# A fixed order on every engine, and local-branch work cut into steps with set lags, in an attention kernel for training

## The chip, the cores and the metric

The kernel runs on one core of a Trainium2 chip. The metric is device time of one execution in microseconds (us). Before the change the median of three runs was 1798.34 us (1797.06 to 1816.73).

Engines in the text: PE multiplies matrices, PEld loads its weights, DVE and ACT do elementwise work, POOL does elementwise work too (adding 128x432 numbers took it 1102 ns, and DVE 603 ns, in the kernel before), and SP issues DMA transfers. PSUM is the memory into which PE writes; the attention phase uses eight of its banks.

## The reference

One encoder block with an attention branch and a local branch (a gated depthwise convolution), forward, and then the gradients of the input and of all seven weights. B = 2, T = 4000, D = 144, five taps, all bf16.

```python
def _fwd_reference(x, w_qkv, w_att_out, w_mlp_in, dw_csgu, w_mlp_out, dw_merge, w_merge):
    xa = _layernorm(x, axis=-1)
    q, k, v = split(xa @ w_qkv)                       # shortened
    p = _softmax(q @ k^T * D ** (-0.5))               # shortened
    glob = (p @ v) @ w_att_out                        # shortened
    h = _gelu(xa @ w_mlp_in)                          # shortened
    u, g = (h[..., :D].copy(), h[..., D:].copy())
    g = _layernorm(g, axis=-1)
    gc = depthwise_conv(g, dw_csgu)                   # 5 taps along T; shortened
    loc = (u * gc) @ w_mlp_out                        # shortened
    ...                                               # merge convolution, projection, residual
# reference(): jax.vjp of this with grad_out; returns the output and eight gradients
```

## The kernel before

Each of the two batches goes through four phases: a head, attention, merge and output, and the gradient of x. One last phase finishes the weight gradients. The change touches the attention phase alone. It goes through 32 rows of 128 tokens, with four *units* per row. A unit makes scores for 1000 columns: eight matmuls into two banks `pS` and two banks `pD`, two exponentials on ACT (`Pm`), two products on DVE (`Sm`). The probabilities and products of older rows are transposed by DMA and multiplied into `y`, and the gradient for the columns is summed through `X` ("fills", two banks, emptied by ACT and POOL or by DVE).

Between these units the kernel runs the local branch, one chain for every pair of rows: `pr`, `ph` (twice), a gelu and norm chain that gives `gn_t`, transposes of it (`pm`, put into `gnC`), a convolution `pc`, transposes of its gradient (`dgC`), the convolution back (`pc` again, read by ACT as `dgf`), and for every two pairs a weight gradient `pw` (twice). **All of these PE steps, and `pj`, which prepares the attention's operands, use the one PSUM bank `ps_f`.** Each must therefore wait until ACT or DVE has emptied the bank of the step before.

```python
def pD(p):                                   # convolution back
    ...
    pc = dgC.conv(p, True)
    for q in range(2):
        nc.scalar.activation(dg[:, q, :], pc[:, q, :], ACT.Copy, scale=rs[:, q:q + 1], accum_out=s12[:, 0, q:q + 1])
    ...
# the local branch is a list of events with times in units; R7 = 7 units per pair
for p in range(NBK // 2):
    t = R7 * p
    ev += [(t, pR, (p,)), (t + 1, pH, (p, 0)), (t + 2, pH, (p, 1)), (t + 2.5, pG, (p,)),
           (t + 9, lambda p: gnC.put(p, gn_t[p]), (p,)), (t + 14, ld_dug, (p,)), (t + 18, pC, (p,)),
           (t + 21, lambda p: dgC.put(p, dgc_t[p]), (p,)), (t + 31, pD, (p,))]
for q in range(NGR):
    ev += [(2 * R7 * q + 24, ld_tap, (q,)), (2 * R7 * q + 31.4, pW, (q, 0)), (2 * R7 * q + 32.4, pW, (q, 1))]
...
# in phase_attn
fills = {(0, 0): 0, (0, 1): 1, (1, 0): 2, (2, 0): 3, (2, 1): 4, (3, 0): 5, (4, 0): 6, (4, 1): 7, (5, 0): 8, (6, 0): 9, (6, 1): 10}
with tc.manual_schedule(engines={mybir.EngineType.PE}):      # PE alone in program order
    for i in range(NBK + 2):
        pr, half = i // 2 - 1, i % 2
        for c2 in range(4):
            if i < NBK:
                unit(i, c2)                  # scores; exponentials and Sm at high priority
            if i < NBK and c2 >= 2:
                flip(i, c2 - 2)              # DMA transposes of P and of Sm
            for place in range(2):
                ...                          # a fill, and at place 0 yz(i - 2, c2)
            if c2 == 3 and i < NBK:
                row_end(i)                   # 1/sum, Qs, br, and Bt
            ...                              # pj at units of its own
            while ev and ev[0][0] < 4 * i + c2 + 1:
                _, fn, a = ev.pop(0)         # all events that are due, one after another
                fn(*a)
```

Only PE follows the program's order here. The order on ACT, DVE, POOL and SP is chosen by a scheduler when the kernel is built.

Of the kernel before, what the change touches and what calls it, by code (L numbers as in the profile page):

```python
# [7 lines left out]
BF = mybir.dt.bfloat16  # L8
# [6 lines left out]
D = 144  # L15
# [1521 lines left out]
def local_steps(k, W, b, S, es, ps):  # L1537
# [9 lines left out]
    R, hs, sq, h_t, gn_t, gp_t, rstd, dug, dgc_t, dh_t, gtap = {}, {}, {}, {}, {}, {}, {}, {}, {}, {}, {}  # L1547
    id_ = W.ident

    def pR(p):  # L1550
        R[p] = wk.tile([128, 256], BF, tag="R", name="R")
        pr = ps.tile([128, 2, 128], BF, tag="f", name="pr")
        for j in range(2):
            nc.tensor.transpose(pr[:, j, :], S.xaa[:, 2 * p + j, 16:D], id_[:])
        nc.scalar.copy(R[p][:], pr[:].rearrange("p a b -> p (a b)"))
        hs[p] = wk.tile([128, 2, 2 * D], BF, tag="hs", bufs=1, name="hs")
        sq[p] = wk.tile([128, 2, 2 * D], BF, tag="sq", bufs=1, name="sq")

    def pH(p, j):
        i = 2 * p + j  # L1560
        ph = ps.tile([128, 2 * D], F32, tag="f", name="ph")
        nc.tensor.matmul(ph[:], S.xaT[:, i * 128:(i + 1) * 128], W.Wi2[:, 0, :], start=True, stop=False)
        nc.tensor.matmul(ph[:], R[p][:, j * 128:(j + 1) * 128], W.Wi2[:, 1, :], start=False, stop=True)
        nc.scalar.copy(hs[p][:, j, :], ph[:])
        nc.scalar.activation(sq[p][:, j, :], ph[:], ACT.Square)
        if j == 1:
            R.pop(p)

    def pG(p):

        h_ = h_t[p] = wk.tile([128, 2, 2 * D], BF, tag="h_t", bufs=4, name="h_t")
        gn_t[p] = wk.tile([128, 2, D], BF, tag="gn_t", bufs=6, name="gn_t")
        gp_t[p] = wk.tile([128, 2, 2 * D], BF, tag="gp_t", bufs=6, name="gp_t")
        rstd[p] = sm.tile([128, 2], F32, tag="rstd", bufs=6, name="rstd")
        x_, s_ = hs.pop(p), sq.pop(p)
        a_ = wk.tile([128, 2, 2 * D], BF, tag="a_", bufs=1, name="a_")
        nc.gpsimd.tensor_scalar(a_[:], s_[:], K0 * K1, K0, op0=ALU.mult, op1=ALU.add)
        nc.vector.tensor_tensor(a_[:], a_[:], x_[:], op=ALU.mult)
        nc.scalar.activation(a_[:], a_[:], ACT.Tanh)
        nc.vector.tensor_scalar(a_[:], a_[:], 0.5, 0.5, op0=ALU.mult, op1=ALU.add)  # L1580
        nc.vector.tensor_tensor(h_[:], a_[:], x_[:], op=ALU.mult)
        norm_rows(k, W, sm, gn_t[p], h_[:, :, D:2 * D], rstd[p], 2, "g")
        t3 = wk.tile([128, 2, 2 * D], BF, tag="t3", bufs=1, name="t3")
        nc.gpsimd.tensor_scalar(t3[:], s_[:], 6 * K0 * K1, 2 * K0, op0=ALU.mult, op1=ALU.add)
        oq = wk.tile([128, 2, 2 * D], BF, tag="oq", bufs=1, name="oq")
        nc.gpsimd.tensor_scalar(oq[:], a_[:], -1.0, 1.0, op0=ALU.mult, op1=ALU.add)
        nc.gpsimd.tensor_tensor(oq[:], oq[:], h_[:], op=ALU.mult)
        nc.vector.tensor_tensor(oq[:], oq[:], t3[:], op=ALU.mult)
        nc.vector.tensor_tensor(gp_t[p][:], oq[:], a_[:], op=ALU.add)
        nc.sync.dma_start(S.gn_d[2 + p * 256:2 + (p + 1) * 256, :].rearrange("(j p) c -> p j c", p=128), gn_t[p][:])  # L1590

    def ld_dug(p):
        dug[p] = wk.tile([128, 2, D], BF, tag="dug", name="dug")
        nc.sync.dma_start(dug[p][:], S.dug_d[:, 2 * p:2 * p + 2, :])

    def ld_tap(q):
        gtap[q] = on.tile([128, 4, 5, D], BF, tag="gtap", name="gtap")
        gn_taps(k, gtap[q], S.gn_d, q, nc.sync)

    def pC(p):  # L1600
        pc = gnC.conv(p, False)
        gc = wk.tile([128, 2, D], BF, tag="gc", bufs=1, name="gc")
        nc.scalar.copy(gc[:], pc[:])
        u_, d_ = h_t.pop(p)[:, :, 0:D], dug.pop(p)
        dgc = dgc_t[p] = wk.tile([128, 2, D], BF, tag="dgc", bufs=4, name="dgc")
        dh_t[p] = wk.tile([128, 2, 2 * D], BF, tag="dh", bufs=3, name="dh")
        ug = wk.tile([128, 2, D], BF, tag="ug", name="ug")
        du = wk.tile([128, 2, D], BF, tag="du", bufs=1, name="du")
        nc.vector.tensor_tensor(dgc[:], d_[:], u_, op=ALU.mult)
        nc.vector.tensor_tensor(du[:], d_[:], gc[:], op=ALU.mult)  # L1610
        nc.vector.tensor_tensor(ug[:], u_, gc[:], op=ALU.mult)
        nc.vector.tensor_tensor(dh_t[p][:, :, 0:D], du[:], gp_t[p][:, :, 0:D], op=ALU.mult)
        nc.sync.dma_start(S.ug_d[:, 2 * p:2 * p + 2, :], ug[:])

    def pW(q, half):

        pw = ps.tile([128, 384], F32, tag="f", name="pw")
        for j in range(4):
            d_ = dgc_t[2 * q + j // 2]
            fl = dict(stop=(j == 3), skip_group_check=True)  # L1620
            if half == 0:
                nc.tensor.matmul(pw[:], d_[:, j % 2, 0:128], gtap[q][:, j, 0:3, 0:128], start=(j == 0), **fl)
            else:
                nc.tensor.matmul(pw[:, 0:256], d_[:, j % 2, 0:128], gtap[q][:, j, 3:5, 0:128], start=(j == 0), **fl)
                nc.tensor.matmul(pw[:, 256:336], d_[:, j % 2, 16:D], gtap[q][:, j, :, 128:D], start=False, **fl)
        w = 384 if half == 0 else 336
        ds = dWs[:, half * 384:half * 384 + w]
        nc.vector.tensor_tensor(ds, pw[:, 0:w], ds, op=ALU.add)
        if half == 1:
            for t in (2 * q, 2 * q + 1):  # L1630
                dgc_t.pop(t)

    def pD(p):
        dh, gn, rs = dh_t.pop(p), gn_t.pop(p), rstd.pop(p)
        s12 = sm.tile([128, 2, 2], F32, tag="s12", name="s12")
        dg = wk.tile([128, 2, D], BF, tag="dgf", name="dgf")
        cc = wk.tile([128, 2, D], BF, tag="cc", bufs=1, name="cc")
        jk = on.tile([128, D], BF, tag="jk", name="jk")
        pc = dgC.conv(p, True)
        for q in range(2):  # L1640
            nc.scalar.activation(dg[:, q, :], pc[:, q, :], ACT.Copy, scale=rs[:, q:q + 1], accum_out=s12[:, 0, q:q + 1])
        for q in range(2):
            nc.vector.scalar_tensor_tensor(jk[:], dg[:, q, :], 1.0, gn[:, q, :], op0=ALU.mult, op1=ALU.mult, accum_out=s12[:, 1, q:q + 1])
        n12 = sm.tile([128, 2, 2], F32, tag="n12", name="n12")
        nc.vector.tensor_scalar(n12[:], s12[:], -1.0 / D, None, op0=ALU.mult)
        for q in range(2):
            nc.gpsimd.tensor_scalar(cc[:, q, :], gn[:, q, :], n12[:, 1, q:q + 1], n12[:, 0, q:q + 1], op0=ALU.mult, op1=ALU.add)
        nc.vector.tensor_tensor(dg[:], dg[:], cc[:], op=ALU.add)
        nc.vector.tensor_tensor(dh[:, :, D:2 * D], dg[:], gp_t.pop(p)[:, :, D:2 * D], op=ALU.mult)
        nc.sync.dma_start(S.dh_d[:, 2 * p:2 * p + 2, :], dh[:])  # L1650

    def taps():
        dc = sm.tile([128, 2, 5], F32, tag="dc", name="dc")
# [6 lines left out]
    ev = []  # L1660
    R7 = 7
    for p in range(NBK // 2):
        t = R7 * p
        ev += [(t, pR, (p,)), (t + 1, pH, (p, 0)), (t + 2, pH, (p, 1)), (t + 2.5, pG, (p,)),
               (t + 9, lambda p: gnC.put(p, gn_t[p]), (p,)), (t + 14, ld_dug, (p,)), (t + 18, pC, (p,)),
               (t + 21, lambda p: dgC.put(p, dgc_t[p]), (p,)), (t + 31, pD, (p,))]
    for q in range(NGR):
        ev += [(2 * R7 * q + 24, ld_tap, (q,)), (2 * R7 * q + 31.4, pW, (q, 0)), (2 * R7 * q + 32.4, pW, (q, 1))]
    ev.append((1e9, taps, ()))
    ev.sort(key=lambda e: e[0])  # L1670
    return ev


def phase_attn(k, W, b, S):
# [3 lines left out]
    with ExitStack() as es:  # L1678
# [20 lines left out]
        def jit(g, step):  # L1699
            r = slice(g * 4, g * 4 + 4)  # L1700
            if step == 0:
                jt[g] = [xp.tile([128, 4, 128], BF, tag=t_, name=t_) for t_ in ("QTm", "BTm", "QBr")]
                for off, src in ((0, S.Q_t), (32, S.B_t), (64, S.Q_t), (96, S.B_t)):
                    nc.gpsimd.tensor_scalar(QB[:, :, off:off + DR], src[:, r, 128:D], 1.0, 0.0, op0=ALU.mult, op1=ALU.add)
            src = (S.Q_t[:, r, 0:128], S.B_t[:, r, 0:128], QB[:])[step]
            pj = ps_f.tile([128, 4, 128], BF, tag="f", name="pj")
            for j in range(4):
                nc.tensor.transpose(pj[:, j, :], src[:, j, :], id_[:])
            nc.scalar.copy(jt[g][step][:], pj[:])
# [25 lines left out]
        def flip(i, h):  # L1735

            pb = i % NP
            for key, src in (("PT", P), ("ST", Sm)):
                t = st[key, i, h] = ab.tile([128, 16, 128], BF, tag=key, bufs=3, name=key)
# [451 lines left out]
```

## Time and profile before

| | before |
|---|---|
| time, median | 1798.34 us |
| attention stage (first exponential to last `X` matmul), first and second batch | 649, 651 us |
| everything else (from the trace's span) | 512 us |
| PE gaps in a stage | 109, 106 us |
| of these ahead of local steps | 91, 89 us |

A gap is the time from the latest end of any matmul or weight load on PE to the next start. I worked the gaps out from the trace's records.

First, five lines of the page of the kernel before. The second is each engine's busy time; the next three are the span in 40 slices with busy shares in tenths, where PEclk is the granted clock in tenths.

```profile
span 1811.2 us, 41290 instructions
...
PE 1401.6 (77%) x15366; PEld 1046.6 (58%) x15366; DVE 917.6 (51%) x3245; ACT 770.1 (43%) x2247; POOL 601.8 (33%) x1179
...
PE   6798877887888789767588877888787878976723
...
PEclk9969998999898999998786998899899989998855
DMA  4267575776675669444526766575577657943420
```

PE is the busiest engine, but in the stages (slices 3 to 16 and 22 to 35) its share is mostly 7 or 8 tenths, and the clock drops here and there. The table of windows says the same for one whole stage and for a quiet piece at its end. Its columns are busy time and instructions of each engine, granted clock, DMA share, and GB/s.

```profile
core 0: us, PE busy (x) PEld busy (x) DVE busy (x) ACT busy (x) POOL busy (x), PEclk, DMA share, GB/s
86.00:736.00 650.00, 539.95 (x5905) 391.02 (x5904) 355.44 (x1134) 318.77 (x944) 233.75 (x449) 0.91 0.68 125
655.00:700.00 45.00, 43.23 (x545) 33.33 (x543) 26.78 (x85) 22.43 (x70) 14.17 (x29) 1.00 0.84 157
```

In the stage PE is busy 540 of 650 us, its weight loads, which overlap, 391, and no other engine more than 355. In 655:700 nothing disturbs it: 43.2 of 45 us. So the other engines can follow at that speed; something else costs the time in the rest of the stage. Now the list of waits of the same kernel. Each line is: who waited, for what, in total us, how many times, the longest.

```profile
engine line waited for: us in total, times, longest us
...
ACT gn_t L1405 <- DVE nm L1403: 96.8, 32, 5.1
...
PE pw L1622 <- ACT dgf L1641: 42.2, 16, 5.0
...
PE ph L1562 <- DVE gnC L1506: 33.2, 30, 2.2
PE pc L1532 <- ACT dgf L1641: 31.8, 8, 4.5
PE pr L1554 <- DVE dgC L1506: 28.8, 26, 2.2
```

All four PE lines are local steps that wait for the shared bank. The timeline shows one such gap of PE, in the kernel before. Columns: start, duration, engine, line, operation, and in brackets the idle time before and what ended it.

```profile
start us, us, engine line op out<-in xcount [idle before <-releaser]
...
303.08 0.17 PE L1533 MATMUL pc<-w_c_482,dgC_4357 80*128 80x16 bf16 x1
308.21 1.12 PE L1622 MATMUL pw<-gtap,dgc 128*128 128x384 bf16 x3 [4.95 <-ACT dgf L1641]
```

### The profile page before, as it was taken

How to read it: one execution, taken by the hardware profiler on the slowest of the kernel's cores; microseconds unless marked ns; L12 is line 12 of the kernel's file. 1: busy time of each engine (PE TensorE's matmuls, PEld its weight loads, DVE VectorE, ACT ScalarE, POOL GpSimd, SP SyncE). 2: the span in 40 equal slices, each digit the busy share in tenths (PEclk: the TensorE clock that was granted, in tenths of full speed). 3: DMA queues.
4: the chain of work that ended last, by engine and by line, in shares of the span. 5: the costliest groups of instructions: out<-in, count | busy, mean ns of one | idle time of the engine just before them, and what ended most of it. 6: DMA issues, size and time to landing. Idle time of an engine off the chain costs nothing. (4 is left out here: it accounts for less than half of the span.)

```text
span 1811.2 us, 41290 instructions
## 1 busy us (share of the span) xinstructions
PE 1401.6 (77%) x15366; PEld 1046.6 (58%) x15366; DVE 917.6 (51%) x3245; ACT 770.1 (43%) x2247; POOL 601.8 (33%) x1179
## 2 busy tenths in 40 slices
PE   6798877887888789767588877888787878976723
PEld 3536555565665567766454655566566656776611
DVE  5455455556555465216635555555555545521653
ACT  4654544555445444111354554455445544411111
POOL 2333343334334333104523343333433433310530
PEclk9969998999898999998786998899899989998855
DMA  4267575776675669444526766575577657943420
GB/s 132 85 110 138 104 138 106 138 130 114 131 131 113 130 124 158 129 113 127 154 67 114 140 114 124 116 135 122 106 142 141 117 109 140 160 127 94 128 92 11
DMA packets 655591, 217.47 MB, mean 120 GB/s; under 512 B 601172, under 2 KB 652308, under 8 KB 655380
## 3 DMA queue, kind: packets, MB, share of 16 engines
q1 hardware_dynamic: 654516, 214.64, 58.3%
q8 instruction: 123, 2.02, 0.5%
q14 instruction: 88, 0.72, 0.1%
q10 hardware_dynamic: 864, 0.09, 0.0%
HBM read 54.74 MB, written 19.88 MB: 41 GB/s over the span
## 5 line engine op out<-in xcount | busy, mean ns | idle before, releaser
L1732 DVE SCALAR_TENSOR_TENSOR Sm<-pD,Pm 128x500 bf16<-128x500 f32 x512 | 326.8, 676 | 242.6 <-ACT Pm L1731 194.3
L1731 ACT ACTIVATE Pm<-pS 128x500 bf16<-128x500 f32 x512 | 295.1, 583 | 138.8 <-PE pS L1726 136.7
L1784 PE MATMUL X<-Qs,Sm 128*128 128x144 bf16 x2048 | 316.5, 236 | 9.8 <-POOL Qs L1754 9.8
L1785 PE MATMUL X<-Bt,Pm 128*128 128x144 bf16 x2048 | 315.4, 236 | 6.0 <-DVE Bt L1757 5.4
L1785 PEld LDWEIGHTS <-Pm 128*128 128x128 bf16 x2048 | 210.6, 103 | 40.0 <-issue 19.3
L1784 PEld LDWEIGHTS <-Sm 128*128 128x128 bf16 x2048 | 211.1, 103 | 37.3 <-issue 15.9
L1726 PE MATMUL pS<-xaT,QTm 128*128 128x500 bf16 x512 | 171.7, 421 | 0.0
L1726 PE MATMUL pD<-xaT,BTm 128*128 128x500 bf16 x512 | 171.1, 419 | 0.0
L1790 POOL TENSOR_TENSOR acc_14480<-xs,acc_14480 128x432 f32<-128x432 f32 x80 | 88.2, 1102 | 248.2 <-ACT xs L1789 248.0
L1790 POOL TENSOR_TENSOR acc_1386<-xs,acc_1386 128x432 f32<-128x432 f32 x80 | 88.1, 1101 | 246.4 <-ACT xs L1789 246.4
L1789 ACT COPY xs<-X 128x432 f32<-128x432 f32 x160 | 82.7, 517 | 188.3 <-PE X L1785 184.6
L1767 PE MATMUL y<-xaa,PT 128*128 128x144 bf16 x2048 | 157.4, 233 | 5.4 <-DVE B_t L1775 5.4
L1767 PE MATMUL y<-xaa,ST 128*128 128x144 bf16 x2048 | 154.3, 230 | 0.0
L1767 PEld LDWEIGHTS <-PT 128*128 128x128 bf16 x2048 | 141.9, 102 | 7.0 <-issue 6.7
L1767 PEld LDWEIGHTS <-ST 128*128 128x128 bf16 x2048 | 139.6, 100 | 6.9
L1722 PE MATMUL pD<-XR,QBr 16*128 16x500 bf16 x512 | 124.9, 412 | 9.1 <-DVE Sm L1732 8.1
L1722 PE MATMUL pS<-XR,QBr 16*128 16x500 bf16 x512 | 116.0, 414 | 6.6 <-ACT Pm L1731 5.3
L1731 ACT ACTIVATION_READ_ACCUMULATOR Pm<-pS 128x1 f32 x512 | 102.9, 201 | 0.0
L1726 PEld LDWEIGHTS <-BTm 128*128 128x128 bf16 x512 | 54.9, 107 | 72.4 <-issue 24.0
L1726 PEld LDWEIGHTS <-QTm 128*128 128x128 bf16 x512 | 29.7, 99 | 86.1 <-issue 86.1
L1792 DVE TENSOR_TENSOR acc_1386<-X,acc_1386 128x432 f32<-128x432 f32 x96 | 55.5, 578 | 42.1 <-PE X L1785 42.0
L1792 DVE TENSOR_TENSOR acc_14480<-X,acc_14480 128x432 f32<-128x432 f32 x96 | 55.5, 578 | 40.6 <-PE X L1785 40.5
(1203 smaller groups left out, 2718.0 us busy)
## 6 DMA issues: line engine op xcount, KB each, us to landing
gs<-in_grad_out_dram SPq DMA_DIRECT2D x24, 720.0 KB
gtap<-gn_d_507 SPq DMA_DIRECT2D x8, 720.0 KB
gtap<-gn_d_13601 SPq DMA_DIRECT2D x8, 720.0 KB
gs<-in_grad_out_dram SPq DMA_DIRECT2D x8, 540.0 KB
xg<-in_x_dram SPq DMA_DIRECT2D x28, 144.0 KB
dh_d_510<-dh SPq DMA_DIRECT2D x16, 144.0 KB
dh<-dh_d_510 SPq DMA_DIRECT2D x8, 288.0 KB
dh_d_13604<-dh SPq DMA_DIRECT2D x16, 144.0 KB
```

The lines of the kernel that those rows point to most:

```text
L1722: nc.tensor.matmul(o_[:, 0:SC], QBr[rr, bi, :], S.XR[rr, c2, 0:SC], start=True, stop=False)
L1726: nc.tensor.matmul(p_[h][:, 0:SC], w_[:, bi, :], S.xaT[:, c0 + h * SC:c0 + (h + 1) * SC], start=False, stop=True)
L1731: nc.scalar.activation(P[:, pb, c1:c1 + SC], pS[h][:, 0:SC], ACT.Exp, accum_out=ld8[:, 0, n:n + 1])
L1732: nc.vector.scalar_tensor_tensor(Sm[:, pb, c1:c1 + SC], pD[h][:, 0:SC], 1.0, P[:, pb, c1:c1 + SC], op0=ALU.mult, op1=ALU.mult, accum_out=l ...
L1767: nc.tensor.matmul(y[:, w, :], src[:, jj, :], S.xaa[:, j, :], start=(j == 0), stop=(j == NBK - 1))
L1784: nc.tensor.matmul(X[:, jj, :], Sm[:, i % NP, j * 128:(j + 1) * 128], Qs[:, i % 4, :], start=(kk == 0), stop=False)
L1785: nc.tensor.matmul(X[:, jj, :], P[:, i % NP, j * 128:(j + 1) * 128], Bt[:, i % 4, :], start=False, stop=(kk == 1))
L1789: nc.scalar.copy(xs[:, 0:nj, :], X[:, 0:nj, :])
L1790: nc.gpsimd.tensor_tensor(a_, xs[:, 0:nj, :], a_, op=ALU.add)
L1792: nc.vector.tensor_tensor(a_, X[:, 0:nj, :], a_, op=ALU.add)
```

## The change

The intent is that PE never meets a bank that is still full. The local chains become generators. Each `yield` says whether a PE step (`P`) or other work (`V`) follows, how many *places* must go by first, and which marks must be passed. A unit has two places, and each place takes at most one `P` step; 149 of 272 places have one. The scheduler is switched off for all engines. This brings smaller moves: the DMA transposes are spread over the units, `Bt` is made after the first unit of the next row, the fills sit at other places, and `pj` goes through the same steps. No arithmetic is added or removed.

The diff, cut to its core (cuts are marked with `# ...`):

```diff
+class Steps:
+    # ... add(), mark(), _ready(), _step()
+    def place(self, tensor=True):
+        again = True
+        while again:
+            again = False
+            for t in list(self.tasks):
+                if (t[1] is None or t[1][0] == 'V') and self._ready(t):
+                    self._step(t)
+                    again = True
+        if tensor:
+            due = [t for t in self.tasks if t[1] is not None and t[1][0] == 'P' and self._ready(t)]
+            if due:
+                self._step(min(due, key=lambda t: t[0]))
+        self.now += 1
 # ... local_steps: pR, pH, pG, pC, pD become one generator
+    def pair(p):
+        # ...
+        yield 'P', 0, aft(("z", 1), ("h", 2))
+        # ... pr, R
+        for j in range(2):
+            yield 'P', 2
+            # ... ph, hs, sq
+        yield 'V', 2, aft(("gp", 1))
+        # ... POOL: a_, t3
+        yield 'V', 2
+        nc.vector.tensor_tensor(a_[:], a_[:], hs[:], op=ALU.mult)
+        yield 'V', 2
+        nc.scalar.activation(a_[:], a_[:], ACT.Tanh)
+        # ... h_t; bn_stats; POOL rstd, each behind a lag of 1 or 2
+        yield 'V', 2, aft(("dh", 6))
+        nc.vector.scalar_tensor_tensor(nm[:], mv[:, :, 0], -1.0, rs[:], op0=ALU.mult, op1=ALU.mult)
+        # ... oq, gp
+        yield 'V', 1
+        # ... ACT: gn_t
+        yield 'P', 2, aft(("gn", 1), ("ug", 2))
+        gnC.put(p, gn)
+        # ... DMA: gn_d, dug
+        yield 'P', 5, # ... after the next gnC
+        pc = gnC.conv(p, False)
+        # ... gc, dgc; then V: ug, du, dh; P: dgC.put; P: conv back and dgf; V, V, V: the rest
 # ... events with times become Q.add(14 * p, pair(p)), Q.add(28 * q + 20, tapcorr(q))
-        def flip(i, h):
-            pb = i % NP
-            for key, src in (("PT", P), ("ST", Sm)):
-                t = st[key, i, h] = ab.tile([128, 16, 128], BF, tag=key, bufs=3, name=key)
-                nc.sync.dma_start_transpose(out=t[:], in_=src[:, pb, h * 2048:(h + 1) * 2048])
+        def flip(key, i, h):
+            t = st[key, i, h] = ab.tile([128, 16, 128], BF, tag=key, bufs=3, name=key)
+            nc.sync.dma_start_transpose(out=t[:], in_=(P if key == "PT" else Sm)[:, i % NP, h * 2048:(h + 1) * 2048])
 # ... row_end without Bt; row_end2(i) makes Bt
-        fills = {(0, 0): 0, (0, 1): 1, (1, 0): 2, (2, 0): 3, (2, 1): 4, (3, 0): 5, (4, 0): 6, (4, 1): 7, (5, 0): 8, (6, 0): 9, (6, 1): 10}
+        fills = {(0, 1): 0, (1, 0): 1, (1, 1): 2, (2, 1): 3, (3, 0): 4, (3, 1): 5, (4, 0): 6, (4, 1): 7, (5, 1): 8, (6, 0): 9, (6, 1): 10}
-        with tc.manual_schedule(engines={mybir.EngineType.PE}):
+        with tc.manual_schedule():
             for i in range(NBK + 2):
                 for c2 in range(4):
                     if i < NBK:
                         unit(i, c2)
+                    if c2 == 0 and 0 <= i - 1 < NBK:
+                        row_end2(i - 1)
                     for place in range(2):
                         # ... a fill
+                        Q.place()
                         # ... yz at place 0; one or two transposes at place 0
-                    while ev and ev[0][0] < 4 * i + c2 + 1:
-                        _, fn, a = ev.pop(0)
-                        fn(*a)
```

## The prediction

> **What bounds it now.** The two attention stages (first to last attention work: 86 to 736 and 941 to 1593 us) are 1302 of 1811 us; the change touches nothing else. The table of windows gives for 86:736: PE busy 540 us (83%), DVE 355, ACT 319, POOL 234, DMA share 0.68, clock 0.91. PE is the bound, but is not kept fed. Its gaps in a stage sum to 109 us, 91 of them (106 and 89 in the second) ahead of local-branch work: pc, pw, ph, pr, pj, pm. All these share one PSUM bank, and two or three are issued in a row at the end of a unit, so each waits for the evacuation of the one before. The list of waits: pw and pc wait for ACT dgf (74 us, up to 5.0 each), ph for the DVE copy of gnC (33), pr for that of dgC (29). Exp starts show units of 3 to 4 us without a collision, 8 to 11.5 with one; the mean is 4.9.
>
> Second cost: [...] the 4.3 to 4.8 us gaps before pc and pw (at 270, 303, 447, 597 us) are followed by 3.4 or 6.8 us at 0.5 clock; 75 us of 150:700 run so, about 38 us lost.
>
> **What the change does.** No arithmetic is added or removed; the order on each engine changes. At most one local TensorE step per place, two places per unit (149 of 272 places used), so the bank has about 2 us to be emptied: ACT hs plus sq need 0.82, gc 0.40, dgf 2 x 0.57. ACT, DVE, POOL and the SP queue follow program order, exps and Sm at the head of each unit. Transposes into PT/ST are spread out, and read at least 5 units after issue. The local chain still ends inside the stage.
>
> **Cost.** PE work per unit: (550 us of 150:700, less 101 of gaps, less 38 of half clock) / 108 units = 3.8 us against 5.1. The window 655:700, where collisions are few, already runs this way: PE 96% busy, clock 1.00, DMA 0.84, so the other engines can follow. In-order ACT (about 2.5 us busy per unit), DVE (2.8) and SP (about 3.5, of it 2.3 per transpose issue) have less slack than before: I allow 0.2 us, thus 4.0 us per unit. A stage: 8 opening units at 3.4, 120 at 4.0, 24 us tail = 532 us against 650. That saves 236 us; I hold some back for new blocking: 218. It is on the critical path, as PE is the bound.
>
> **Predicted: 1580 us, 1530 to 1650.** Faster by over 2%: 0.93; within: 0.05; slower: 0.02.
>
> **Signs.** Right: PE's gaps before local work fall from 180 us to under 40; units even, at 3.7 to 4.4 us; clock in the stage above 0.95 after its opening; PE above 92%; DMA share 0.8 or more; other stages unchanged. Wrong: PE waiting in front of pS/pD for Sm (DVE late, its Sm delayed by in-order local work), for X banks, or y for PT/ST.
>
> **What would make it wrong.** A DVE or SP queue blocked at its head by one late producer, so that a fixed order turns jitter into stalls of everything; DMA saturating (3.5 us of 16-engine time per unit), so transposes land late; then 1650 or more. If in-order costs less than I allow: 1540.

The four gaps named are in the trace, and each was followed by 6.8 us at half clock. The 38 us are an estimate, half of the 75 us at half clock; 8 × 3.4 + 120 × 4.0 + 24 comes to 531, given as 532 us a stage; and 1798 less 218 is 1580.

## More of the kernel before

```profile
303.32 0.38 ACT L1641 ACTIVATE dgf<-pc,rstd 128x144 bf16<-128x144 f32 x1 [0.87 <-PE pc L1533]
...
306.90 0.90 ACT L1405 ACTIVATE gn_t<-h_t,nm,rstd 128x144 bf16<-128x144 bf16 x2 [3.11 <-DVE nm L1403]
307.71 0.36 ACT L1641 ACTIVATE dgf<-pc,rstd 128x144 bf16<-128x144 f32 x1
```

In the gap of PE shown above, ACT reads the first half of the bank at 303.32. The second half was ready too (PE's last matmul of `pc` ended at 303.25), but on ACT `gn_t` comes between the two. It waits 3.11 us for `nm` of DVE, and the second `dgf` comes behind it, at 307.71, although the trace shows nothing else that holds it back. The trace has 18 gaps of PE over 3 us in the two stages, 74 us in all. In every one of them ACT does `gn_t` before the read that ends the gap; in 16 that is `dgf`, in the other two `BTm`, another read of the same bank. In 12 of the 18 two exponentials run in the gap as well.

## The result

| | before | after |
|---|---|---|
| time, median (lowest to highest, runs) | 1802.92 us (1797.06 to 1816.73, 4) | 1618.01 us (1616.32 to 1623.41, 4) |
| ratio, 95% interval | 1 | 0.897 (0.891 to 0.9029) |
| attention stages | 649, 651 us | 555, 553 us |
| everything else | 512 us | 506 us |
| PE gaps in a stage | 109, 106 us | 46, 46 us |
| of these ahead of local steps | 91, 89 us | 20, 20 us |
| at half clock in a stage, after its first 36 us | 82, 92 us | 24, 14 us |
| unit (first exponential to the next), median; 10th to 90th percentile | 4.4; 3.1 to 8.3 us | 4.0; 3.3 to 5.6 us |

The kernel is faster by 10%. All outputs are right. A ratio in this document is the mean time of one kernel's runs over that of the other's in the same rounds, so it is not quite the ratio of the medians that stand beside it.

The page of the kernel after, the lines that answer to those above:

```profile
span 1614.5 us, 41127 instructions
...
PE 1337.2 (83%) x15366; PEld 1009.7 (63%) x15366; DVE 920.8 (57%) x3245; ACT 762.2 (47%) x2247; POOL 591.5 (37%) x1179
...
PE   5899899899898989767579989989898998876723
...
PEclk9959999999999999979686999999999999997855
DMA  5358888887888679444526887898887887843420
```

The counts of matmuls, DVE and ACT instructions are those of before. Inside the stages PE is at 8 to 9 tenths nearly everywhere. The windows of the kernel after show a whole stage, and its middle:

```profile
86.00:641.00 555.00, 509.26 (x5900) 373.77 (x5898) 358.11 (x1140) 315.14 (x947) 231.06 (x457) 0.95 0.81 146
120.00:600.00 480.00, 436.32 (x5228) 329.29 (x5226) 318.25 (x997) 279.87 (x838) 208.68 (x419) 0.98 0.82 149
```

The same instructions took 509 us of busy PE instead of 540, since less of the stage ran at half clock. A matmul took longer there: in the kernel before the record of an `X` matmul is 327 ns in the median at half clock and 226 ns at full clock, and the starts of successive ones are 0.12 us apart from 277.97 to 279.29 (half clock) and 0.06 us from 280.55 to 280.99 (full clock). The waits of the kernel after:

```profile
PE X L1856 <- DVE Bt L1828: 36.0, 29, 1.7
...
PE X L1855 <- POOL Qs L1819: 10.3, 14, 3.1
...
PE ph L1615 <- DVE dgC L1506: 8.7, 10, 1.5
...
ACT gn_t L1659 <- DVE nm L1651: 4.2, 8, 0.7
```

The waits of `pw` and `pc` for `dgf` are gone, ACT waits 4.2 us for `nm` instead of 96.8, and the longest in the PE lines shown is 3.1 us instead of 5.0. A new first line has come up: `X` waits 36 us for `Bt`.

**Where the 197 us came from.** I split each stage in three: the gaps of PE; the loss to half clock (an estimate: half of the half-clock time that lies outside gaps, as those starts were twice as far apart; counted after the first 36 us of the stage, which are alike in both kernels: 30 us at half clock in the first stage and 32 in the second); and the rest, which is PE at work. For the first stage before: 649 − 109 − (82 − 7)/2 = 502 us. For that of after the rest is 499. So of the 96 us that a stage saves on average, 62 are gaps (108 to 46) and about 30 are half clock; PE's own work moved by 3. Other phases gave 6 us in the whole kernel.

In these two traces half clock mostly came after gaps. After the first 36 us of a stage it comes in stretches of 3.4 or 6.8 us, 43 in the four stages; in the 8 us ahead of 40 of them a gap of over 1 us began. Each of the 18 gaps over 3 us in the kernel before was followed by half clock within 5.3 us of its start. Shorter gaps were followed by it too: in the kernel before one of 2.54 us at 378.4 by half clock at 382.1, and one of 2.22 us at 543.6 by half clock at 545.9; in the kernel after gaps of 1.66, 1.46 and 2.81 us (at 344.7, 484.7 and 433.9) each by 3.4 us at half clock. Of the 31 gaps of 1.3 to 1.7 us in the stages of both kernels, 24 were not followed by half clock within 7.5 us of their start.

### The profile page after: what moved, and what is told of

It reads as the page before. It is cut to its first block, busy times and chain, and to the rows that moved or that the text cites. A ratio compares the mean times of both kernels' runs of the same rounds, so it can differ in the third digit from the quotient of the medians. Undisturbed runs are those within 1.5% of the kernel's fastest.

```text
span 1614.5 us, 41127 instructions
## 1 busy us (share of the span) xinstructions
PE 1337.2 (83%) x15366; PEld 1009.7 (63%) x15366; DVE 920.8 (57%) x3245; ACT 762.2 (47%) x2247; POOL 591.5 (37%) x1179
## 5 line engine op out<-in xcount | busy, mean ns | idle before, releaser
L1856 PE MATMUL X<-Bt,Pm 128*128 128x144 bf16 x2048 | 297.3, 227 | 36.1 <-DVE Bt L1828 36.0
L1855 PE MATMUL X<-Qs,Sm 128*128 128x144 bf16 x2048 | 299.0, 227 | 10.3 <-POOL Qs L1819 10.3
L1855 PEld LDWEIGHTS <-Sm 128*128 128x128 bf16 x2048 | 202.0, 99 | 54.3 <-issue 41.2
L1856 PEld LDWEIGHTS <-Pm 128*128 128x128 bf16 x2048 | 201.7, 98 | 26.9 <-issue 13.2
L1796 PE MATMUL pS<-xaT,QTm 128*128 128x500 bf16 x512 | 162.3, 401 | 0.0
L1796 PE MATMUL pD<-xaT,BTm 128*128 128x500 bf16 x512 | 159.6, 395 | 0.0
L1838 PE MATMUL y<-xaa,PT 128*128 128x144 bf16 x2048 | 153.6, 230 | 0.8 <-DVE B_t L1846 0.8
L1838 PE MATMUL y<-xaa,ST 128*128 128x144 bf16 x2048 | 148.8, 226 | 0.0
L1838 PEld LDWEIGHTS <-ST 128*128 128x128 bf16 x2048 | 132.6, 98 | 6.5
L1792 PE MATMUL pD<-XR,QBr 16*128 16x500 bf16 x512 | 121.1, 396 | 4.8 <-DVE Sm L1802 4.3
```

What stands on the lines that cost most here:

```text
L1792: nc.tensor.matmul(o_[:, 0:SC], QBr[rr, bi, :], S.XR[rr, c2, 0:SC], start=True, stop=False)
L1796: nc.tensor.matmul(p_[h][:, 0:SC], w_[:, bi, :], S.xaT[:, c0 + h * SC:c0 + (h + 1) * SC], start=False, stop=True)
L1838: nc.tensor.matmul(y[:, w, :], src[:, jj, :], S.xaa[:, j, :], start=(j == 0), stop=(j == NBK - 1))
L1855: nc.tensor.matmul(X[:, jj, :], Sm[:, i % NP, j * 128:(j + 1) * 128], Qs[:, i % 4, :], start=(kk == 0), stop=False)
L1856: nc.tensor.matmul(X[:, jj, :], P[:, i % NP, j * 128:(j + 1) * 128], Bt[:, i % 4, :], start=False, stop=(kk == 1))
```

## The experiments

The question: the change did two large things at once. Theory **P** (places): one local step per place leaves time to empty the shared bank; the order of the other engines matters little. Theory **F** (fixed order): placement is secondary, and what counts is that ACT, DVE, POOL and SP now follow the program, so that urgent evacuations no longer stand behind work that is not ready. Later runs ask which engine's order it is (**D**: DVE's), and whether neither half works without the other (**C**).

This table has all runs. Those named e1 to e12 come from three sessions on three chips (e1 to e4, e5 to e8, e9 to e12), and each ratio is to the kernel before in the same session. Stage, gaps and so on are means of the two stages of that kernel's profile, in us, worked out as above. "local" are the gaps ahead of local steps and `pj`, "scores" those ahead of `pS` and `pD`, "X" those ahead of the fills.

| kernel | median | ratio to before (95%) | stage | gaps | local | scores | X | half clock | rest |
|---|---|---|---|---|---|---|---|---|---|
| before | 1803 to 1810 | 1 | 650 | 108 | 90 | 7 | 8 | 87 | 503 |
| after | 1618.0 | 0.897 (0.891–0.9029) | 554 | 46 | 20 | 2 | 23 | 19 | 500 |
| e1 after, PE alone fixed | 1728.19 | 0.954 (0.9492–0.9589) | 608 | 71 | 38 | 27 | 1 | 67 | 508 |
| e2 before, four fixed | 1994.44 | 1.102 (1.097–1.1069) | 739 | 172 | 101 | 62 | 9 | 169 | 506 |
| e3 after, both places at end | 1717.62 | 0.9495 (0.9452–0.9538) | 604 | 80 | 53 | 2 | 25 | 44 | 504 |
| e4 before, `dgf` first | 1814.76 | 1.0027 (0.9981–1.0072) | 652 | 106 | 63 | 22 | 15 | 82 | 510 |
| e5 after, `Bt` early | 1620.26 | 0.8981 (0.8952–0.9009) | 554 | 42 | 29 | 5 | 7 | 17 | 504 |
| e6 after, fills later | 1607.75 | 0.8909 (0.8878–0.8939) | 548 | 38 | 29 | 7 | 1 | 19 | 502 |
| e7 after, PE and DVE fixed | 1613.13 | 0.8926 (0.8889–0.8963) | 550 | 42 | 26 | 3 | 12 | 19 | 500 |
| e8 after, PE and ACT fixed | 1706.43 | 0.9442 (0.9404–0.948) | 596 | 59 | 23 | 31 | 0 | 60 | 510 |
| e9 before, PE and DVE fixed | 1896.03 | 1.0494 (1.0471–1.0517) | 695 | 133 | 68 | 56 | 9 | 124 | 508 |
| e10 e6 and e7 together | 1608.28 | 0.8907 (0.8884–0.8929) | 547 | 38 | 32 | 5 | 1 | 21 | 500 |
| e11 e10, SP fixed too | 1602.04 | 0.888 (0.8852–0.8908) | 546 | 36 | 30 | 5 | 1 | 21 | 500 |
| e12 after, unchanged | 1618.13 | 0.8975 (0.8947–0.9003) | 554 | 46 | 20 | 2 | 24 | 17 | 500 |

The columns to look at together are "stage" and "rest". From the fastest to the slowest kernel the stage goes from 546 to 739 us, and the rest stays between 500 and 510. PE's own work is the same in all of them; they differ only in how long PE stands still, and in how long it runs at half clock: 17 to 21 us where the gaps are 36 to 46 us, 82 to 169 where they are 106 to 172.

### e1: only the placement

```diff
-        with tc.manual_schedule():
+        with tc.manual_schedule(engines={mybir.EngineType.PE}):
```

> The kernel after, but only PE keeps the program order; ACT, DVE, POOL and the SP queue go back to the scheduler. Theory P (the gain comes from where the local TensorE steps stand, so that the one shared PSUM bank has time to be emptied): most of the gain stays, 1600 to 1670 us, and the PE gaps before local steps stay under 80 us for both stages. Rival F (the gain comes from the fixed order of the other engines, above all that ACT gets to the evacuations in time): most is lost, 1720 to 1810 us, and gaps of 3 to 5 us before pc and pw return.

Measured: 1728.19 us, ratio 0.954. The time is just inside F's range, and P as the only cause falls. But F's sign did not come: no gap of 3 us before `pc`, and one before `pw`. The local gaps are down as P says (90 to 38 a stage, under 80 for both stages), but the scores now wait. So neither theory holds alone. Two lines from the waits of e1:

```profile
PE pD L1792 <- DVE Sm L1802: 45.7, 66, 4.4
...
DVE dgc L1671 <- DMA dug<-dug_d: 85.5, 28, 6.4
```

And one case from its timeline, DVE and then PE:

```profile
305.47 0.31 DVE L1671 TENSOR_TENSOR dgc<-dug,h_t 128x288 bf16<-128x288 bf16 x1 [6.41 <-DMA dug<-dug_d]
305.70 0.67 DVE L1802 SCALAR_TENSOR_TENSOR Sm<-pD,Pm 128x500 bf16<-128x500 f32 x1
```

```profile
301.68 0.38 PE L1792 MATMUL pS<-XR,QBr 16*128 16x500 bf16 x1
306.43 0.48 PE L1792 MATMUL pD<-XR,QBr 16*128 16x500 bf16 x1 [4.37 <-DVE Sm L1802]
```

The scheduler put `dgc` ahead of the product `Sm` on DVE. `dgc` waits 6.41 us for a DMA, `Sm` stands behind it, its `pD` bank stays full, and PE waits 4.37 us. This is the pattern of the kernel before (there ACT, `gn_t` and `dgf`), on another engine. In the kernel after, `dgc` does not appear among the waits for a DMA at all.

### e2: only the fixed order

The kernel before, with ACT, DVE and POOL in program order as well as PE. SP could not be included: that version deadlocks when it is built. So does a version of the kernel after with the old transposes, in which a transpose would have to wait for a `yz` further on in the program. So spreading the transposes belongs to fixing SP's order, and could not be tried apart from it.

```diff
-        with tc.manual_schedule(engines={mybir.EngineType.PE}):
+        with tc.manual_schedule(engines={PE, Activation, DVE, Pool}):      # names shortened
```

> The kernel before with its places as they are, but PE, ACT, DVE and POOL in program order (the SP queue stays with the scheduler: in program order too, the transposes into PT and ST deadlock on their three buffers). Theory P: steps still stand in a row on one bank, so 1760 us or more, or slower than before because long local chains now stand in one piece in front of the exps on ACT and DVE. Rival F: the evacuations come in time, 1620 to 1720 us.

Measured: 1994.44 us, ratio 1.102. F as the only cause falls too: at the old places, fixed order makes the kernel 10% slower. The waits of e2:

```profile
PE pw L1622 <- ACT dgf L1641: 70.0, 16, 9.8
PE pD L1722 <- DVE Sm L1732: 63.9, 27, 3.4
PE pS L1722 <- ACT Pm L1731: 59.3, 20, 4.5
```

Each chain of the old program is written in one piece, so in program order it blocks ACT and DVE for as long as the chain takes to pass through the engines: in e2 ACT's `gn_t` waits 99.5 us for `nm`, and DVE 86.0 us for POOL's `oq` (19.7 in the kernel before).

### e3: the steps, but not spread over the unit

The kernel after, with both steps of a unit at its end.

```diff
-                        Q.place()
+                        if place == 1:
+                            Q.place()
+                            Q.place()
```

> The kernel after with both places of a unit at its end, one straight after the other: as many local steps in a unit, the same fixed order, but two of them can meet at the bank again. Theory P: gaps before local steps grow from about 35 us to 100 us or more in both stages together (about 1 us for each pair that meets), 1660 to 1720 us. Rival F: within 1% of the kernel after, 1605 to 1635 us.

Measured: 1717.62 us, ratio 0.9495, and the local gaps of both stages together rise from 40 to 105 us. By the ratios this costs 95 us. In the traces the two stages are 99 us longer: 65 of them are local gaps and 23 half clock. The order of all engines is fixed as in the kernel after, but `Q.place()` also carries the `V` steps, so these stand together at the unit's end too: the run shows what spreading both kinds of steps is worth, not PE's steps alone.

### e4: the visible wait alone, in the kernel before

The largest waits of PE before the change were for `dgf`. Here the scheduler is told to rank `dgf` first; nothing else is touched.

```diff
+        with tc.high_priority():
             for q in range(2):
                 nc.scalar.activation(dg[:, q, :], pc[:, q, :], ACT.Copy, scale=rs[:, q:q + 1], accum_out=s12[:, 0, q:q + 1])
```

> The kernel before with one edit: ACT's evacuation of the backward convolution (dgf) gets the priority of the exps. My prediction said that ACT reached dgf late because the scheduler ranked it behind other work. If that is so, the 74 us of pc and pw waiting for dgf shrink to under 25, half-clock time in the stages shrinks with them, and the kernel takes 1690 to 1750 us. If dgf was late for another reason (data or the bank), 1785 to 1815.

Measured: 1814.76 us, ratio 1.0027 (0.9981 to 1.0072): the same. It is not that the edit missed. The waits of `pw` and `pc` for `dgf` fell from 74 to 20.2 us, under the 25 that was expected, and the gaps ahead of all local steps from 90 to 63 us a stage. (The expectation says that my prediction gave the scheduler's rank as the reason for the late `dgf`; the prediction does not.) But the waits of e4 show three others grown, each of which was under 10 us in the kernel before, beside the one that fell:

```profile
PE X L1785 <- POOL Qs L1755: 23.2, 10, 4.5
PE pD L1723 <- DVE Sm L1733: 23.0, 37, 2.8
...
PE pw L1622 <- ACT dgf L1642: 20.2, 16, 2.7
PE pS L1723 <- ACT Pm L1732: 20.1, 10, 2.6
```

The gaps sum to 106 us a stage as before. With one instruction moved forward, others came late.

### e5 and e6: the new wait of the kernel after

`X` waits 36 us for `Bt`. In e5, `Bt` is made ahead of the next row's first unit instead of after it. In e6, `Bt` stays and the first three fills move one place away from it.

```diff
 # e5
-                    if i < NBK:
-                        unit(i, c2)
                     if c2 == 0 and 0 <= i - 1 < NBK:
                         row_end2(i - 1)
+                    if i < NBK:
+                        unit(i, c2)
 # e6
-        fills = {(0, 1): 0, (1, 0): 1, (1, 1): 2, (2, 1): 3, (3, 0): 4, ...
+        fills = {(1, 0): 0, (1, 1): 1, (2, 0): 2, (2, 1): 3, (3, 0): 4, ...
```

> The kernel after with one edit: row_end2 (DVE writes Bt) is called before the first unit of the next row instead of after it, so on DVE it stands before that unit's two Sm and not behind them. Theory B (the gaps in front of X, 36 us in the two stages, exist only because Bt stands behind two Sm of 0.6 us that wait for exps not yet run): the X waits for Bt fall from 36 to under 10 us and the time falls by 15 to 35 us, 0.978 to 0.99 of the kernel after, 1583 to 1603 us. Rival (Bt is late because its inputs Qs and br come late, or the wait only moves to the following pD): X waits move to Qs or pD, time within 0.6% of the kernel after.

> The kernel after with the first four X fills one place later, so that none stands in the first unit after a row's end; Bt stays where it is. Theory B: the X waits for Bt fall under 10 us here as well. But the first unit of such a row then gives PE less to do while ACT and DVE work on its exps and Sm, so some of the gain should come back as waits of pD for Sm: 1590 to 1612 us. If the place of the fills matters more than Bt, slower than 1618.

Measured: e5 1620.26 us, ratio 0.8981, no gain; e6 1607.75 us, ratio 0.8909 (0.8878 to 0.8939). Both took the wait for `Bt` away: the wait of 36 us fell to 3 in e5, and the gaps ahead of `X` from 23 to 1 us a stage in e6. In e5 the 16 us a stage that left the fills came back: 9 at the local steps, 3 at the scores, 4 in the rest. In e6 they took part of it back as well. The waits of e5, then of e6:

```profile
PE pw L1718 <- DVE dgC L1506: 12.9, 10, 2.6
...
PE pD L1792 <- DVE Sm L1802: 10.2, 30, 2.1
```

```profile
PE pw L1718 <- DVE dgC L1506: 24.2, 10, 4.7
...
PE pD L1792 <- DVE Sm L1802: 10.6, 42, 0.5
```

In the kernel after, these lines were 7.5 and 4.3 us. The 36 us of waiting for `Bt` were for the most part slack in which the other engines caught up. e6 against e12 (0.8975, 0.8947 to 0.9003, in another session, each against the kernel before) is a gain of 0.7%. (The expectation of e6 speaks of four fills; the edit moves three.)

### e7, e8 and e9: which engine's order

e7 and e8 are the kernel after with PE and DVE, or PE and ACT, in program order, the other engines left to the scheduler. e9 is the kernel before with PE and DVE in program order.

```diff
-        with tc.manual_schedule():
+        with tc.manual_schedule(engines={PE, DVE}):          # e7; e8: {PE, Activation}
 # e9, in the kernel before
-        with tc.manual_schedule(engines={PE}):
+        with tc.manual_schedule(engines={PE, DVE}):
```

> The kernel after with only PE and DVE in program order, ACT, POOL and SP with the scheduler. In the first run of this kind (PE alone, 1728 us) the longest PE gap was pD waiting for Sm on DVE, 46 us in both stages, and the bank's copies on DVE. Theory D (DVE's order is the part of the fixed order that counts): 1630 to 1670 us and pD waits under 15 us. Rival A (ACT's order counts): 1700 to 1730.

> The kernel after with only PE and ACT in program order, DVE, POOL and SP with the scheduler. Theory D: little comes back, 1690 to 1730 us, with pD waits for Sm still 35 us or more. Rival A: 1630 to 1670 us.

> The kernel before, its places as they are, with PE and DVE in program order: the fourth corner beside before (PE alone), the PE-alone and the PE-and-DVE run of the kernel after. Theory C (a fixed DVE order pays only because the change also cut the local chains into small steps with lags; as one piece a chain stands in front of the next Sm and waits there for other engines): no gain or a loss, 1790 to 1950 us, with pD waits for Sm of 40 us or more. Rival D (a fixed DVE order is worth about 115 us by itself, as it was at the new places): 1660 to 1720 us.

Measured: e7 1613.13 us, ratio 0.8926, better than any theory expected and as fast as all engines fixed (0.8889 to 0.8963 against 0.8947 to 0.9003 of e12). e8 1706.43 us, ratio 0.9442. e9 1896.03 us, ratio 1.0494. So DVE's order is the one that counts, and ACT's is worth one point (0.954 to 0.9442). In e8 it is again `Sm` that comes late, and DVE's `dgc` waits 53.7 us for its DMA, as in e1. One line of the waits of e8:

```profile
PE pD L1792 <- DVE Sm L1802: 61.3, 79, 3.6
```

With e1 this makes a square:

| ratio to before | PE alone fixed | PE and DVE fixed |
|---|---|---|
| old places, chains in one piece | 1 | 1.0494 (e9) |
| new places, chains in steps | 0.954 (e1) | 0.8926 (e7) |

The same switch costs 5 points in the upper row and gains 6 in the lower one: that is what C says. The rows differ in the whole of the rest of the change, though (places, steps with lags, fills, `Bt`, transposes); steps at the old places, or whole chains at the new ones, were not run. That it is the chains is read from the trace of e9. Two lines of its waits, with the second as it was in the kernel before, then its DVE and its PE at one of these places:

```profile
PE pD L1722 <- DVE Sm L1732: 109.8, 41, 5.6
...
DVE nm L1403 <- POOL rstd L1401: 75.7, 32, 3.0
```

```profile
DVE nm L1403 <- POOL rstd L1401: 34.4, 32, 1.7
```

```profile
285.62 0.18 DVE L1398 BATCH_NORM_AGGREGATE mv<-st 128x2 f32<-128x6 f32 x1
288.75 0.16 DVE L1403 SCALAR_TENSOR_TENSOR nm<-mv,rstd 128x2 f32<-128x2 f32 x1 [2.95 <-POOL rstd L1401]
...
289.81 0.68 DVE L1732 SCALAR_TENSOR_TENSOR Sm<-pD,Pm 128x500 bf16<-128x500 f32 x1
```

```profile
290.55 0.57 PE L1722 MATMUL pD<-XR,QBr 16*128 16x500 bf16 x1 [4.91 <-DVE Sm L1732]
```

The old chain asks DVE for `mv`, POOL for `rstd` and DVE for `nm` in one piece. In program order DVE stands 2.95 us until POOL is done, with `Sm` behind it. In the steps of the change, `nm` comes two places after POOL's work, so DVE does not meet it before it is ready: this wait does not appear in the kernel after.

### e10, e11 and e12: both gains, and the kernel after beside them

e10 is e6 with PE and DVE fixed; e11 fixes SP as well. e12 is the kernel after, unchanged, on the same chip.

```diff
+        fills = {(1, 0): 0, (1, 1): 1, (2, 0): 2, (2, 1): 3, (3, 0): 4, ...
+        with tc.manual_schedule(engines={PE, DVE}):          # e11: {PE, DVE, SP}
```

> The two edits that looked a little better than the kernel after, together: X fills one place later, and only PE and DVE in program order. If their gains add: 0.985 to 0.993 of the kernel after run beside it. If both only move the same waits about: within 0.5% of the better one of the two, about 0.993 of the kernel after.

> As the run before, with the SP queue in program order as well. With PE and DVE alone, pc waited 19 us for the small DMAs of gnC, which the kernel after does not show (3 us): if that is the scheduler's order on the SP queue, these waits fall under 8 us here and the time falls by 5 to 15 us, to 0.98 to 0.988 of the kernel after. If they come from ACT or POOL being late, they stay and so does the time.

> The kernel after unchanged, as the reference on the same chip for the small differences in this call: 0.895 to 0.90 of the kernel before, 1612 to 1624 us.

Measured: e10 1608.28 us, ratio 0.8907, which is e6 again: the two gains do not add. e11 1602.04 us, ratio 0.888 (0.8852 to 0.8908), which is 0.989 of e12 and so just misses the 0.98 to 0.988 expected. e12 1618.13 us, ratio 0.8975. The waits of e10, then of e11, show what SP's order does:

```profile
PE pc L1533 <- DMA gnC<-gnC: 18.5, 9, 4.4
```

```profile
PE pc L1533 <- DMA dgC<-dgC: 6.1, 4, 2.6
...
PE pc L1533 <- DMA gnC<-gnC: 3.6, 4, 1.6
```

With SP left to the scheduler, the small copies inside SBUF that the convolution reads come late: `pc` waits 18.9 us for both kinds in e10 (0.4 of it for `dgC`) and 9.7 in e11. The time fell little, and e10 and e11 are not told apart by their intervals. Both beat the kernel after, and e11 is the fastest of all that ran: 1% under the kernel after, 11% under the kernel before.

## Why the prediction was right, and where it was not

The prediction was 1580 us in 1530 to 1650, with 0.93 on faster. It came to 1618 us: faster, within the range, 38 us above the point.

- **What bounds it: right, with part of the cause missing.** PE, kept waiting by local steps on one bank. After the change the gaps ahead of local steps are 40 us for both stages instead of 180, on the line of "under 40". But the prediction puts the waits down to steps in a row alone; 74 of the 180 us are the gaps over 3 us, in which `gn_t` stands ahead in ACT's queue.
- **PE's work per unit, 3.8 us: right.** It gave 27 us for eight opening units, 120 × 3.8 and 24 for the tail, thus 507 us a stage (an estimate). The rest column measures 500 to 510 in every kernel.
- **The half clock: right.** Clock in 120:600 is 0.98; above 0.95 was predicted. It is a third of the gain.
- **Other stages unchanged: right**, 512 and 506 us. DMA share 0.82: right (0.8 or more).
- **PE above 92%: just missed**, 436 of 480 us is 91%. **Units even, at 3.7 to 4.4 us: missed.** The median is 4.0, but the 10th to 90th percentile is 3.3 to 5.6.
- **The wrong sign that was named came up in another form.** I named waits for X banks. No wait of `X` for a bank shows among the waits of the kernel after; `X` waited for `Bt`, 36 us. e5 and e6 show that this was mostly slack.

**The step that failed** is "In-order ACT ..., DVE ... and SP ... have less slack than before: I allow 0.2 us". It is wrong in size, and wrong in kind.

In size: 0.2 us for 120 units are 24 us a stage. Measured are 46 us of gaps and about 9 us of half clock, thus 0.46 us a unit. Against 507 + 24, rounded to 532, the stage took 554. The opening, tail and unit work were 7 us better than I had them, and the allowance was 30 us too small. Twice the 22 us that remain are 44; less the 18 that I held back on purpose and the 6 that other phases gave, that is 20 of the 38 us. The other 18 come mostly from a mismatch: I took the saving from a profile whose span was 1811 us and subtracted it from the median of 1798.

In kind: I took the fixed order for a price to be paid for the places. But with the scheduler's order, too, work that was ready came behind an instruction that waited, and that order was just another fixed one, with worse blocks in it (ACT's `gn_t` in the kernel before, which waited 96.8 us in all, DVE's `dgc` in e1, 85.5 us). With DVE left to the scheduler the same places give only 0.954. Fixing DVE's order takes that to 0.8926, which is more than half of the whole gain. In the kernel before, the same switch loses 5 points. I did name "a DVE or SP queue blocked at its head by one late producer" as a danger of the change; e1 shows it as a danger of leaving the scheduler in charge, and e9 as a danger of a fixed order with chains in one piece.

What made the sum come out nearly right is that I took the unit time as PE's own work, with all gaps and half clock subtracted, and so did not have to know which of the two parts would take them away. That was partly luck: the places, to which the prediction credits the whole gain, give 0.954 without the fixed order (e1).

**What stays open.** Why the last 36 us of gaps a stage resist: e5, e6, e7, e10 and e11 each removed a named wait, and most of the time came back as other waits. In e11 the largest wait left inside the stages is again one for the shared bank: `pw` for `dgC`, 23.1 us for both stages, against 7.5 in the kernel after. And what the spread of the transposes does by itself: it could not be separated from SP's order without a deadlock.

## What to carry to other kernels

Whoever orders an engine's work, for each instruction that empties a bank ask which instruction stands just ahead of it and what that one waits for: here it was `gn_t` ahead of `dgf`, with waits of up to 5.1 us for `nm` (kernel before), and `dgc` ahead of `Sm`, with waits of up to 6.4 us for a DMA (e1). In this kernel fixed program order paid only together with chains across engines cut into steps, each issued late enough for its input to be ready (0.954 to 0.8926 with DVE's order fixed); with chains in one piece the same switch made things worse (1.0494 in e9, and 1.102 in e2). Moving up a single visible wait can gain nothing (e4, e5): count the sum of the gaps before and after, not the one line.
